# Attention and two feed-forward layers in one kernel: load times, longer waits for other engines, an early table load and an earlier verdict in the order of side work

## The chip, the cores and the metric

One Trainium2 chip, one of its cores. The time is device microseconds (us) of one launch, the median of several runs. Engines are named as in the profile: PE is TensorE's matmul and PEld its weight load, DVE is VectorE, ACT is ScalarE, POOL is GpSimd, SP is SyncE, whose queue issues the loads and stores.

## What is computed

Soft-capped attention (2 batches, 12 heads, 448 positions, 64 per head), then a feed-forward layer with relu squared (768 to 2048 to 768) on 896 tokens, then another of the same size with silu. All inputs are float32.

```python
scores = scale * np.matmul(q, k.transpose(0, 1, 3, 2))
scores = cap * np.tanh(scores / cap)
scores = scores - np.max(scores, axis=-1, keepdims=True)
attn = np.exp(scores)
attn = attn / (np.sum(attn, axis=-1, keepdims=True) + 1e-09)
x = np.matmul(attn, v)                      # then to (896, 768)
h = x @ w_in;   r = np.maximum(h, 0.0);  x = (r * r) @ w_out
h = x @ w2_in;  g = h * (1.0 / (1.0 + np.exp(-h)));  out = g @ w2_out
```

## The kernel before

**Two ways through.** `run(attention_bounded, "f", F16)` computes all of it with feed-forward operands split into a float16 high and low part, and takes samples on the way that tell whether that was good enough (`Watch`). `Watch.judge` puts them together on DVE (eight small operations, lines 244 to 251), `Watch.add_up` sums over partitions with a small matmul (line 254) and three DVE operations (255 to 257) to one number, `ok`. Each engine reads it into a register (`values_load`, line 1337, an instruction TENSOR_LOAD on each of the five). Only if it is not 1 does a second, general program run.

**Attention** (to about 86 us) fills TensorE with float32 products, ACT with tanh and exp.

**The feed-forward layers.** A layer's first product is w_in ("a" in layer one, "c" in layer two), its second w_out ("b", "d"). Each product is three float16 matmuls: high by high, high by low, low by high. Weights come as *words*: tiles of 128 x 768 float64 numbers (768 KB) loaded by SP into three raw buffers (`load_to`, line 275). A word is *turned* into float32 (`turn_steps`): ACT (POOL for the first four) copies the top half into a buffer of zeros (`head`, line 339), DVE shifts the rest under it (`shift`, line 342), and the shift's end lets SP load word i + 3 into the raw buffer. The zeros buffers are three: one for words 0 to 7, two in turn for the others. Then a word is *split* into high (ACT, line 366) and low (DVE, line 206) in a slot `hl`; there are 13 slots, the last three in a pool that opens after attention. Most products of four blocks use seven multiplications in place of eight (`Pair`, and the last stage of layer two, lines 1289 to 1338): sums and differences of words and of operands are formed on DVE (lines 391, 846), and the products go p1, p5, p6, p2, p7, p3, p4. p6 and p2 wait for the copy k1 of p1's bank, p7 for the copy or sum k2 of p6's, p3 for k5. The first pair of layer two goes in another order (`first`), with p7 straight behind p6. The first four columns of layer one (`plain`) use eight.

**Who decides the order.** [...] Program order on ACT and DVE is made at build time by a planner (`Stream`): a `Step` has an engine, a cost from its columns, steps that it depends on, a gate and a due time. TensorE's work moves a clock (`chunk`), and while an engine's planned clock lies behind it, the open step with the earliest due time is put out, of the urgent ones (`late`) or the first six of the background (`bg`). The copies and sums that free a bank (`ends`) are put out when their product is. `open` takes a step whose dependencies on other engines ended HOP = 0.21 us ago by the plan. The plan knows neither the weights' loads nor the reload of the activation table, and starts all engines at 0 when attention ends (`begin`). What TensorE wants and isn't yet put out is forced (`need`, `run_first`).

**Last stage of layer two.** Two groups of two pairs each. Sums go into `yf`, which holds layer two's first results, loaded back from a spill in DRAM (line 1248) as soon as layer two's input is no longer read. The judgement stands behind p7 of the last group, the small matmul and the read behind p3.

Of the kernel before, what the change touches and what calls it, by code (L numbers as in the profile page):

```python
# [26 lines left out]
def softcap_attention_relu2_silu(  # L27
# [12 lines left out]
    nc = tc.nc  # L40
# [139 lines left out]
    HOP = 0.21  # L180
    SLACK = 0.3

# [76 lines left out]
    class Stream:  # L259


        def __init__(self, plan, tag, wpool, dt, watch):
            self.todo = plan
            self.tag, self.wpool, self.dt, self.watch = tag, wpool, dt, watch
            self.nslots, self.nwords, self.nraw = (10, 4, 3) if watch else (5, 4, 3)
            self.nrests = 4 if watch else NHR
            self.nfirst, self.nslots = self.nslots, self.nslots + (3 if watch else 0)
            self.raw, self.hl, self.ready, self.freed = [], {}, {}, {}
            self.turned, self.slots, self.rests, self.order, self.u = [], [], [], [], {}
            self.words, self.read = [], {}  # L270
            self.bg, self.late = {"A": [], "D": [], "P": []}, []
            self.clock, self.now = {"A": 0.0, "D": 0.0, "P": 0.0}, 0.0
            self.steps, self.done = self.plan(), []

        def load_to(self, i):
            while len(self.raw) < min(i + 1, len(self.todo.items)):
                src, name = self.todo.items[len(self.raw)]
                raw = self.wpool.tile([128, WT * 8], I8, tag="raw", bufs=self.nraw, name=f"raw_{name}{self.tag}")
                nc.sync.dma_start(raw, src)
                self.raw.append(raw)  # L280

        def slot(self, i):
# [36 lines left out]
        def turn_steps(self, i):  # L319

            k = 0 if i < 8 or not self.watch else 1 + i % 2
            before = [j for j in range(i) if (0 if j < 8 or not self.watch else 1 + j % 2) == k]

# [4 lines left out]
            def top():  # L330
                return zeros[:, 0] if k == 0 else self.zeros[:, k - 1]

# [16 lines left out]

            a = Step("P" if i < 4 else "A", 280 if i < 4 else 1.4 * WT, head, [self.turned[j] for j in {*before[-1:], *range(max(0, i - self.nraw), max(0, i - self.nraw + 1))}])  # L350
            b = Step("D", WT, shift, [a], self.room)
# [84 lines left out]
        def begin(self):  # L436
# [4 lines left out]
            for st in self.steps:  # L441
                self.bg[st.eng].append(st)
            self.clock = dict.fromkeys(self.clock, 0.0)
            for st in self.done:
                st.end = 0.0

        def run(self, st):
            for d in st.deps:
                if d.end is None:
                    self.run_first(d)  # L450
            t = max([self.clock[st.eng]] + [d.end + (HOP if d.eng != st.eng else 0) for d in st.deps])
            st.fn()
            st.end = self.clock[st.eng] = t + st.cost
# [11 lines left out]
        def open(self, st, now, eng):  # L465
            if any(d.end is None or d.end + (HOP if d.eng != eng else 0) > now for d in st.deps):
                return False
# [383 lines left out]
    def feed_forward(ws, x0, x1_of, ytile, gpool, qpool, tag, dt, power, ones):  # L851
# [324 lines left out]
        for ph in range(len(phases["a"])):  # L1176
# [7 lines left out]
            if ph == len(phases["a"]) - 1:  # L1184
                x1 = x1_of(ws, y1)

            def seed1(acc, n, u):
# [22 lines left out]
        for ph in range(len(phases["c"])):  # L1210
# [93 lines left out]
            for es, p in [(es, p) for es in groups for p in ("p1", "p2", "p5", "p6", "p7", "p3", "p4")]:  # L1304
                for m, e in [(m, e) for m in range(MN) for e in es]:
# [22 lines left out]
                    else:  # L1328
                        ws.chunk(UNIT / 4)
                if p == "p7" and es == groups[-1]:  # L1330
                    for i in (ws.todo.where["d", 0, e] for e in es):
                        ws.get((i, "r"))
                    ws.finish()
                    watch.judge(capt)
                if p == "p3" and es == groups[-1]:
                    watch.add_up(ones[0], bank("judge"))
                    verdict.append(nc.values_load(watch.ok.bitcast(I32), min_val=0, max_val=0x3F800000))
        ws.finish()
# [135 lines left out]
    def run(attention, tag, dt):  # L1474
        narrow = dt == F16
        power = POWER if narrow else dict.fromkeys(POWER, 0)
        with ExitStack() as pools:
# [34 lines left out]
            if watch:  # L1512
                ws.zeros = gpool.tile([128, 2, WT], I32, tag="zeros", name=f"zeros{tag}")
                nc.gpsimd.memset(ws.zeros, 0)
# [59 lines left out]
```

## Time and profile before

| what | us |
|---|---|
| median of 3 runs | 515.94 |
| lowest, highest | 513.95, 517.15 |
| the profiled execution's own time | 513.88 |
| its span, first to last instruction | 512.0 |
| PE busy in it | 493.8 |
| DVE, ACT, POOL busy | 389.4, 344.9, 32.7 |

A row of the timeline gives start, length, engine, line, operation, what it writes and reads, and in brackets how long its engine stood idle before it and which instruction's end let it go. Buffer numbers are left out of some names: `zerosf<-raw_wa5f` is the top half of word 5 of w_in, `hl_51f` a slot's 51st use, `p_6df` a bank of the last stage's second group. A busy PE counts a matmul from start to end, and matmuls overlap.

### The profile page before, as it was taken

To read this page: it belongs to the slowest core of one execution; us is meant where nothing else is said; L and a number is where in the kernel's file an instruction comes from. 1 tells how busy PE (TensorE), PEld (TensorE's weight loads), DVE (VectorE), ACT (ScalarE), POOL (GpSimd) and SP (SyncE) were. 2 spreads that over 40 slices of the span, in tenths; PEclk is the share of its full clock that TensorE was granted. 3 is DMA by queue.
4 is the path that set the end of the run, shared out by engine and by line. 5 is a ranking of instruction groups with operands and counts; after the bars stand their busy time and mean duration, and the time that the engine had idled before them with its cause. 6 is when DMAs were issued, how large, how long until landed. Compare 5 with 4: busy or idle time off the path is not lost.

```text
span 512.0 us, 7109 instructions
## 1 busy us (share of the span) xinstructions
PE 493.8 (96%) x2608; PEld 237.6 (46%) x2608; DVE 389.4 (76%) x754; ACT 344.9 (67%) x540; POOL 32.7 (6%) x33
## 2 busy tenths in 40 slices
PE   8999999998999999999999997999999999998994
PEld 4233333454545555555555554455555555554551
DVE  0888999989989998457988977787043289988853
ACT  6999896679689984249887679897243487871200
POOL 1103554300000000000000000000000000000000
PEclk9999999999999999999999999999999999999999
DMA  7756553333356745515241114653335132232023
GB/s 250 259 151 172 181 155 96 98 140 137 125 184 222 238 158 181 189 51 196 91 156 62 63 61 133 231 192 123 116 115 180 55 123 64 61 124 92 2 100 122
DMA packets 22386, 69.76 MB, mean 136 GB/s; under 512 B 2886, under 2 KB 14150, under 8 KB 22342
## 3 DMA queue, kind: packets, MB, share of 16 engines
q1 hardware_dynamic: 22308, 69.22, 40.7%
q8 instruction: 22, 0.36, 0.3%
q14 instruction: 22, 0.18, 0.1%
q0 software_dynamic: 32, 0.00, 0.0%
q10 hardware_dynamic: 2, 0.00, 0.0%
HBM read 63.64 MB, written 5.54 MB: 135 GB/s over the span
## 4 chain that ended last, share of the span: by engine, by line
PE 69%; DVE 15%; ACT 8%; DMA 5%; issue 2%; SPq 0%; DVEq 0%; ACTq 0%
PE px L623 4%; PE p_6df L896 3%; PE yb_1f L896 3%; PE yb_4f L896 3%; PE yb_0f L896 3%; PE yb_5f L896 3%; PE yb_2f L896 3%; PE yb_3f L896 3%; PE s_A L604 2%; PE p_4df L896 2%; DMA yf<-spill 2%; PE yd_3f L896 2%; PE yd_2f L896 2%; PE yd_5f L896 2%; PE yd_4f L896 2%
## 5 line engine op out<-in xcount | busy, mean ns | idle before, releaser
L612 ACT ACTIVATE e_B<-s_B 128x896 f32<-128x896 f32 x18 | 15.9, 917 | 4.1 <-PE s_B L604 3.8
L612 ACT ACTIVATE e_A<-s_A 128x896 f32<-128x896 f32 x18 | 15.9, 918 | 3.7 <-PE s_A L604 3.4
L708 ACT ACTIVATE e_B<-e_B 128x896 f32<-128x896 f32 x18 | 16.5, 954 | 0.0
L708 ACT ACTIVATE e_A<-e_A 128x896 f32<-128x896 f32 x18 | 16.5, 955 | 0.0
L1254 DVE SCALAR_TENSOR_TENSOR yf<-p_6df,yf 128x448 f32<-128x448 f32 x15 | 9.2, 623 | 7.7 <-PE p_6df L896 7.7
L206 DVE SCALAR_TENSOR_TENSOR hl_63f<-u_62f,hl_63f 128x768 f16<-128x768 f32 x1 | 1.0, 958 | 17.4 <-ACT hl_63f L366 17.4
L643 DVE TENSOR_TENSOR total<-total,e_C 64x896 f32<-64x896 f32 x11 | 12.9, 1172 | 0.4
L206 DVE SCALAR_TENSOR_TENSOR hl_67f<-u_67f,hl_67f 128x768 f16<-128x768 f32 x1 | 1.0, 958 | 14.3 <-ACT hl_67f L366 14.3
L639 DVE TENSOR_TENSOR total<-total,e_A 128x896 f32<-128x896 f32 x6 | 8.8, 1472 | 0.3
L206 DVE SCALAR_TENSOR_TENSOR x1f<-yaf,x1f 128x448 f16<-128x448 f32 x12 | 7.4, 620 | 2.2 <-ACT x1f L835 2.2
L1254 DVE SCALAR_TENSOR_TENSOR yf<-p_4df,yf 128x448 f32<-128x448 f32 x15 | 8.9, 613 | 0.0
L835 ACT ACTIVATE x1f<-yaf 128x448 f16<-128x448 f32 x11 | 6.2, 568 | 3.8 <-DVE yaf L846 3.7
L846 DVE TENSOR_TENSOR yaf<-yaf 128x448 f32<-128x448 f32 x12 | 7.2, 621 | 1.2 <-ACT yaf L835 1.1
L339 ACT ACTIVATE zerosf<-raw_wb_7f 128x768 f16<-128x768 bf16 x2 | 2.1, 1074 | 7.9 <-DMA raw_wb_7f<-in_moe_w_out 4.2
L637 DVE TENSOR_TENSOR total<-e_A,e_A 128x896 f32<-128x896 f32 x6 | 6.6, 1101 | 0.6 <-ACT e_A L708 0.6
L835 ACT ACTIVATE ycf<-yd_4f 128x448 f32<-128x448 f32 x2 | 1.1, 543 | 8.0 <-PE yd_4f L896 8.0
L637 DVE TENSOR_TENSOR total<-e_B,e_B 128x896 f32<-128x896 f32 x5 | 6.5, 1293 | 0.0
L835 ACT ACTIVATE ycf<-yd_0f 128x448 f32<-128x448 f32 x2 | 1.1, 543 | 7.8 <-PE yd_0f L896 7.8
L896 PEld LDWEIGHTS <-hl_5f 128*128 128x128 f16 x36 | 3.5, 97 | 5.8 <-issue 2.8
L696 DVE RECIPROCAL r<-r 128x448 f32<-128x448 f32 x2 | 5.9, 2952 | 0.1
L896 PE MATMUL p_6df<-yformsf,hl_78f 128*128 128x448 f16 x18 | 4.4, 352 | 1.6 <-DVE ok L257 1.6
L366 ACT ACTIVATE hl_79f<-u_79f 128x768 f16<-128x768 f32 x1 | 0.8, 843 | 7.4 <-DVE u_79f L342 7.4
(1836 smaller groups left out, 1653.7 us busy)
## 6 DMA issues: line engine op xcount, KB each, us to landing
spill<-ycf SPq DMA_DIRECT2D x12, 224.0 KB, 1.9
yf<-spill SPq DMA_DIRECT2D x12, 224.0 KB, 5.3
out<-yf SPq DMA_DIRECT2D x12, 224.0 KB, 2.0
rb<-scratch SPq DMA_DIRECT2D x10, 224.0 KB, 4.0
raw_wb_0f<-in_moe_w_out SPq DMA_DIRECT2D x2, 768.0 KB, 5.8
raw_wb_1f<-in_moe_w_out SPq DMA_DIRECT2D x2, 768.0 KB, 4.4
raw_wb_2f<-in_moe_w_out SPq DMA_DIRECT2D x2, 768.0 KB, 6.8
raw_wb_3f<-in_moe_w_out SPq DMA_DIRECT2D x2, 768.0 KB, 5.5
```

The source lines that it names most:

```text
L206: nc.vector.scalar_tensor_tensor(lo, x, scale, hi, op0=ALU.mult, op1=ALU.subtract, accum_out=watch.low() if see else None)
L604: nc.tensor.matmul(sp[:, j, :S] if b is None else sp[head(b), j, :S], lhsT=qk[head(j), 1, 128 * c : min(128 * c + 128, S)], rhs=qk[head(j) ...
L612: nc.scalar.activation(t, sp[:, :, :S], AF.Tanh, scale=scale_s)
L623: nc.tensor.matmul(px[i][head(j), :S], lhsT=v_m[:, 3 * j + int(x[1])] if b is None else pr.vc[m][head(b), j], rhs=e[:, j] if b is None els ...
L637: nc.vector.tensor_tensor(t, ex[m, x[0] + "0"], e, op=ALU.add)
L639: nc.vector.tensor_tensor(total[i], total[i], e, op=ALU.add)
L643: nc.vector.tensor_tensor(t, t, ex[m, "C"][head(b)], op=ALU.add)
L708: nc.scalar.activation(ex[m, x], ex[m, x], AF.Exp, scale=scale_c)
L835: return Step("A", cols, lambda: nc.scalar.activation(at(out), at(src), func, scale=scale), list(deps))
L846: return Step(eng, cols, lambda: e.tensor_tensor(at(out), at(x), at(y), op=op), list(deps))
L896: nc.tensor.matmul(acc, lhsT=w(e_w, kk), rhs=x(e_x, kk), start=first and i == 0, stop=last and i == len(n) - 1, skip_group_check=more,)
L1254: return Step("D", S, lambda: nc.vector.scalar_tensor_tensor(yb, acc, to_y, yb, op0=ALU.mult, op1=ALU.add), list(deps))
```

## The change

Seven edits, all to the planner's knowledge or to where a step stands:

- `loaded`: each load gets a time at which the plan expects it, 4.5 us after the step that issued it and at least 3.1 us after the load before; the copy of a top half has it as its gate.
- CAUTION: `open` asks for 0.6 us, not 0.21, since a dependency on another engine ended.
- `begin` starts DVE's clock at 2.2. `run` lets a step's planned start wait for its gate.
- Zeros buffers: two in all. Odd words from 9 on use the second, the others the first.
- Slots: 14 in place of 13, four in the late pool, in the room that the zeros buffer gave up.
- A silu activation of one element is put out as a late ACT step in layer one's last phase, before its output products.
- `judge` moves behind p5 of the last group (with the splits that it wants), `add_up` behind p6, the read behind p7.

```diff
-    SLACK = 0.3
+    SLACK, CAUTION = 0.3, 0.6
+    LOAD, NEXT_LOAD = 4.5, 3.1
...
-            self.nfirst, self.nslots = self.nslots, self.nslots + (3 if watch else 0)
+            self.nfirst, self.nslots = self.nslots, self.nslots + (4 if watch else 0)
...
+                last = self.loaded[-1] if self.loaded else 0.0
+                self.loaded.append(max(self.at + LOAD, last + NEXT_LOAD) if self.loading else -1.0)
...
-            k = 0 if i < 8 or not self.watch else 1 + i % 2
-            before = [j for j in range(i) if (0 if j < 8 or not self.watch else 1 + j % 2) == k]
+            k = i % 2 if i > 7 and self.watch else 0
+            before = [j for j in range(i) if k == (j % 2 if j > 7 and self.watch else 0)]
...
+            def loaded():
+                return self.loaded[i] if i < len(self.loaded) else -1.0 if i < self.nraw else None
...
-            a = Step("P" if i < 4 else "A", 280 if i < 4 else 1.4 * WT, head, [self.turned[j] for j in {*before[-1:], *range(max(0, i - self.nraw), max(0, i - self.nraw + 1))}])
+            a = Step("P" if i < 4 else "A", 280 if i < 4 else 1.4 * WT, head, [self.turned[j] for j in {*before[-1:], *range(max(0, i - self.nraw), max(0, i - self.nraw + 1))}], loaded)
...
-            self.clock = dict.fromkeys(self.clock, 0.0)
+            self.clock = {"A": 0.0, "D": 2.2, "P": 0.0}
...
+            if st.gate is not None:
+                t = max(t, st.gate() or 0.0)
+            self.at = t + st.cost
...
-            if any(d.end is None or d.end + (HOP if d.eng != eng else 0) > now for d in st.deps):
+            if any(d.end is None or d.end + (CAUTION if d.eng != eng else 0) > now for d in st.deps):
...
+                ws.later(Step("A", 1400, lambda: nc.scalar.activation(warm, warm, AF.Silu)))
...
-                if p == "p7" and es == groups[-1]:
+                if p == "p5" and es == groups[-1]:
                     for i in (ws.todo.where["d", 0, e] for e in es):
-                        ws.get((i, "r"))
+                        ws.need(ws.ready[i + 1], ws.ready[i, "r"])
                     ws.finish()
                     watch.judge(capt)
-                if p == "p3" and es == groups[-1]:
+                if p == "p6" and es == groups[-1]:
                     watch.add_up(ones[0], bank("judge"))
+                if p == "p7" and es == groups[-1]:
                     verdict.append(nc.values_load(watch.ok.bitcast(I32), min_val=0, max_val=0x3F800000))
...
-                ws.zeros = gpool.tile([128, 2, WT], I32, tag="zeros", name=f"zeros{tag}")
+                ws.zeros = gpool.tile([128, WT], I32, tag="zeros", name=f"zeros{tag}")
```

## Rows read from the trace of the kernel before

**Rows 1.** The page: busy time by engine, and the chain that ended last
```profile
PE 493.8 (96%) x2608; PEld 237.6 (46%) x2608; DVE 389.4 (76%) x754; ACT 344.9 (67%) x540; POOL 32.7 (6%) x33
PE 69%; DVE 15%; ACT 8%; DMA 5%; issue 2%; SPq 0%; DVEq 0%; ACTq 0%
```

**Rows 2.** Stage table: stretch, then per engine busy us (x instructions); clock; DMA
```profile
84.00:152.00 68.00, 63.81 (x333) 31.89 (x330) 62.78 (x120) 53.50 (x94) 5.69 (x6) 1.00 0.43 145
406.00:458.00 52.00, 52.00 (x277) 26.89 (x275) 47.38 (x117) 41.33 (x72) 0.00 (x0) 1.00 0.24 79
```

**Rows 3.** TensorE's waits: for whom, us in total, times, longest
```profile
PE ac0f L896 <- ACT u2c0f L835: 2.7, 1, 2.7
PE p_6df L896 <- DVE ok L257: 1.6, 1, 1.6
PE p_4df L896 <- DVE yf L1254: 1.5, 2, 1.3
PE aa4f L896 <- ACT ca4f L835: 1.2, 1, 1.2
PE ha_0f L896 <- ACT ha_0f L835: 1.1, 1, 1.1
PE yb_0f L896 <- DVE ga3f L206: 0.8, 1, 0.8
PE yb_0f L896 <- ACT ga3f L835: 0.6, 1, 0.6
PE yb_1f L896 <- DVE ga3f L206: 0.5, 1, 0.5
```

**Rows 4.** Timeline, first layer: start, us, engine, line, tiles [idle before <-releaser]
```profile
86.53 2.44 PE L896 MATMUL ha_0f<-x0f,hl_0f 128*128 128x448 f16 x12
...
95.21 0.58 ACT L835 ACTIVATE x0f<-x_c11f 128x448 f16<-128x448 f32 x1 [4.53 <-DVE x_c11f L697]
...
114.53 1.07 ACT L339 ACTIVATE zerosf<-raw_wa5f 128x768 f16<-128x768 bf16 x1 [2.82 <-DMA raw_wa5f<-in_moe_w_in]
...
138.72 1.08 ACT L339 ACTIVATE zerosf<-raw_wa9f 128x768 f16<-128x768 bf16 x1 [2.24 <-DMA raw_wa9f<-in_moe_w_in]
```

**Rows 5.** Timeline, first pair of layer two
```profile
306.81 0.84 ACT L366 ACTIVATE hl_51f<-u_51f 128x768 f16<-128x768 f32 x1 [1.57 <-PE cc0f L896]
...
307.56 0.35 PE L896 MATMUL ac0f<-x_c11f,hl_39f 128*128 128x448 f16 x1
...
307.66 1.28 ACT L835 ACT_TABLE_LOAD   x1
...
308.95 0.54 ACT L835 ACTIVATE c11c0f<-cc0f 128x448 f32<-128x448 f32 x1
...
310.01 0.53 ACT L835 ACTIVATE u2c0f<-ac0f 128x448 f32<-128x448 f32 x1
```

**Rows 6.** Timeline around the verdict, VectorE and TensorE
```profile
490.49 0.63 DVE L1254 SCALAR_TENSOR_TENSOR yf<-p_6df,yf 128x448 f32<-128x448 f32 x1 [0.51 <-PE p_6df L896]
...
493.69 0.73 PE L896 MATMUL p_6df<-yformsf,hl_78f 128*128 128x448 f16 x3
...
497.84 0.13 DVE L244 TENSOR_SCALAR signs<-capt 1x1 f32<-1x1 f32 x1
...
499.59 0.16 DVE L251 TENSOR_TENSOR squares<-squares,within 128x1 f32<-128x1 f32 x1
```

**Rows 7.** Line 1337, the verdict's read: count, duration in ns min/median/max, first and last start
```profile
L1337 PEldq TENSOR_LOAD <-ok x1: 712/712/712, 501.7 to 501.7; - x1
```

**Rows 8.** Timeline of VectorE: a split that waits for its slot, a sum for the spill
```profile
376.92 0.96 DVE L206 SCALAR_TENSOR_TENSOR hl_63f<-u_62f,hl_63f 128x768 f16<-128x768 f32 x1 [17.39 <-ACT hl_63f L366]
...
462.88 0.62 DVE L1254 SCALAR_TENSOR_TENSOR yf<-c_4df,yf 128x448 f32<-128x448 f32 x1 [4.08 <-DMA yf<-spill]
```

**Rows 9.** Stage table of line 206 alone (lower halves and their reads), VectorE
```profile
406.00:458.00 52.00, 23.34 (x72) 1.00 0.24 79
458.00:484.00 26.00, 8.55 (x22) 1.00 0.24 82
```

More of the change, by code (lines that the diff above doesn't have):

```diff
@@ L270, in __init__ @@
             self.words, self.read = [], {}
+            self.loaded, self.at = [], 0.0
             self.bg, self.late = {"A": [], "D": [], "P": []}, []
@@ L330, in top @@
             def top():
-                return zeros[:, 0] if k == 0 else self.zeros[:, k - 1]
+                return zeros[:, 0] if k == 0 else self.zeros
+            def loaded():
+                return self.loaded[i] if i < len(self.loaded) else -1.0 if i < self.nraw else None
             def head():
```

## The prediction

> **What bounds the kernel now.** I read the page first (busy shares and the chain that ended last), then the stage table, then the list of what TensorE waited for, and then the timeline around each of these waits. TensorE is busy 96% of the span and the chain is TensorE for 69% [rows 1]; its granted clock is 1.00 in every stage quoted [rows 2], so no term below is one of the clock. A gain can only come out of TensorE's idle time and of the tail. The list of its waits says where that idle time is: after attention, eight entries of 0.5 us or more hold 10.0 us [rows 3]. They are 2.7 (first pair of layer two), 1.6 (the verdict), 1.5 (the last stage), 1.2 (the first paired products), 1.1 and 0.8 + 0.6 + 0.5 = 1.9 (first layer's plain products). No entry is for a weight split. The change works on the order in which ScalarE (ACT) and VectorE (DVE) get side work, so its worth is the sum of what becomes of these eight, less new waits that another order makes.
>
> **First layer, start: 1.1 and 1.9 us.** TensorE begins the layer at 86.53. ACT, next in order with x0f, stands idle 4.53 us until DVE's last normalisation lets it go at 95.21 [rows 4]. The planner took DVE as free at 0: by its own costs 0.55 + 2.90 + 0.55 + 0.21 it had x0f ready at 4.2, and the trace has it at 95.21 - 86.53 = 8.7. With DVE set to 2.2 it is planned at 6.4, so some 2.2 of the 4.53 us should be filled with work that now stands behind it. The wait of 1.1 us [rows 3] is for a bank whose relu is queued behind; 2.2 us more is enough: 1.1 gained. Next, ACT stands 2.82 us before the top half of word wa5, whose load has not landed, and the relus for ga2 and ga3 are behind it [rows 4]. TensorE's 1.9 us of waits for ga3 follow. The new gate plans that half for 4.5 us after the load's issue, so relus go first. It could give back all 1.9, or nothing if DVE, which is busy 62.78 of 68 us in this stage [rows 2], is what is late (two of the three waits name DVE); I take 1.5. **Sum 2.6, from 1.1 to 3.0.** A loss from words turned later I leave out here, as no wait now is for a weight.
>
> **First paired products: 1.2 us.** The copy ca4f is late after ACT has lost 2.24 us to the load of wa9 [rows 4]. The same gate removes it; but DVE's words for the same ACT work are as late, so I take **0.9, from 0 to 1.2**.
>
> **Silu's table: 2.68 us.** The load takes 1.28 us and runs while TensorE waits for u2c0f; before it ACT waited 1.57 us for cc0f and then did hl_51f, 0.84 us [rows 5]. hl_51f takes the buffer of word 38 (13 slots), which is read until cc0f is done; with 14 slots it takes that of word 37, free earlier. If only the table load goes, u2c0f ends 1.28 us sooner. If hl_51f goes too, u2c0f is bound by the product's end: last matmul 307.56 + 0.35 = 307.91, some 0.02 to start, 0.53 for the copy, 0.05 to restart, a wait of about 0.64, thus 2.04 gained. I take **1.6, from 1.28 to 2.04**. At its new place, behind the first layer's last products, the load costs ACT the same 1.28 us and a one-element activation. The output products that follow read words and g tiles made before, and want the last pair's g only eight units on: that hides it. Without this cover it would cost TensorE 1.28 us there. It issues no DMA.
>
> The trace shows no pause between hl_51f's end (306.81 + 0.84), the load at 307.66 and the silu at 308.95: a switch costs 1.28 us [rows 5]. The Trainium skill (ScalarE: Activation LUTs, What ACT_TABLE_LOAD costs) has 1283 ns for the load, which agrees, and a DRAIN of about 1380 ns beside it, which this trace doesn't show; by its 2.66 us this term would be 2.66 and 1.06 more than I take. The row decides.
>
> **Verdict: 1.6 us.** Now judge starts when the p7 sums are done (497.84), ends at 499.59 + 0.16 = 499.75, and TensorE waits for the verdict behind its sum [rows 6]. After, it starts behind the third p5 sum, 490.49 + 0.63 = 491.12, and by the same 1.91 us ends at 493.03. What is late next: the p6 sums queued behind it on DVE. The first would end at 493.03 + 0.62 = 493.65, and p7's first product, which wants it, starts at 493.69 now; the sum's small matmul stands before it, so I see it as just in time (up to 0.5 us lost if not). Behind three sums of 0.62 the verdict is ready near 495, over two us before p7's sums are done (497.84 now), where each engine reads it. That read takes TensorE's queue 0.712 us [rows 7] and nothing covers it but what is already in the array. 1.6 - 0.7 = **0.9, from 0.4 to 1.6**. DVE's own read falls between p7's and p3's sums, where no product waits for it; SP's stands before the p3 stores, which are not due before their sums; ACT and POOL have nothing left behind it. The tail after the last matmul is unchanged.
>
> **Fourteenth slot, last stage: 1.5 us.** DVE stood 17.39 us for hl_63f, whose slot was held by words of layer two's first output stage, and in the last stage TensorE waits for sums while DVE does weight splits as long as that one, 0.96 us; there DVE had stood 4.08 us for the spill's load, which the planner doesn't know before or after [rows 8]. One slot more lets one split go into that idle time: **0.5, from 0 to 0.96**. The second zeros buffer that pays for it was one of three; the first is now used on, so word 8 waits for word 7, in a stretch with room.
>
> **New waits.** A changed greedy order makes some. The trace has nothing that prices them but its own: 10.0 / 8 = 1.25 us each; I take one of 0.9, between that and the smallest (0.5); from 0 up to the slower rival. The caution of 0.6 us has no instruction of its own.
>
> **Sum.** 2.6 + 0.9 + 1.6 + 0.9 + 0.5 = 6.5; less 0.9 = 5.6 us. Against the profiled execution, 513.88 us (its span 512.0 and 1.9 around it), that is 508.3. That execution is at the low edge of the runs (513.95 to 517.15); taken off their median of 515.94 it gives **510.3 us**, my forecast. If all goes to its upper end: 3.0 + 1.2 + 2.0 + 1.6 + 1.0 = 8.8, with no new wait: 507.1.
>
> **The rivals.**
> - All upper ends: 507.1, or a little under with the rest of the waits. Chance 0.08.
> - The waits for loads only move: ACT does relus first, but then turned words come late, and DVE, at 62.78 of 68 us, is the bound of the first layer. Then only table and verdict are left, 1.6 + 0.9 = 2.5: 513.4. For it: two of the three ga3 waits name DVE. Against: ACT's idle time comes before the relus that DVE waits for. Chance 0.21.
> - The table load does not stay away. If Relu isn't in silu's set, the relus still open at the new place bring the first table back, and silu's load returns at 307. The term of 1.6 is lost: 511.9. In this trace Copy and Square run in both layers with no reload; of Relu under silu's table it shows nothing. Chance 0.07. (The Trainium skill, ScalarE: Activation LUTs, Table sets, says relu and copy are in every set: by that the rival falls.)
> - Slower: DVE starves in layer two's second half. From 406 to 458 it is busy 47.38 of 52 us, so 4.6 are free [rows 2], and 36 of its steps there (72 instructions with their reads) follow an ACT step [rows 9]. The caution holds each back by up to 0.6 - 0.21 = 0.39 us in the plan; where DVE then gets a sum that waits for TensorE in its place, that time is lost. All 36 lose 14.0 us, and with the 11 such steps from there to 484, where DVE's idle time lies behind the spill's load, 18.3; less 4.6 free, less 6.0 gained by the other terms: 7.7 slower, 523.6. It decides against the change from (4.6 + 6.0) / 0.39 = 27 steps on, and by more than 1% (5.2 us) from 41. Against it: the caution moves a plan, not an instruction, and DVE mostly has other work. Chance 0.12.
>
> **How the numbers follow.** The forecast as told (net gain of some 3.5 to 8) has 0.52. What a measurement of this kernel can tell from no change is about 1%, 5.2 us: faster by more means under 510.8, and the forecast is just there. Of its 0.52 I put 0.41 under that line and 0.11 within 1%. Faster: 0.41 + 0.08 = 0.49. Same: 0.11 + 0.21 + 0.07 + 0.04 of the last rival = 0.43. Slower: 0.08, the rest of it. The range reaches from 506, the upper ends and the runs' own spread, to 516.5, which takes in the second and third rivals and leaves the slower one out; the forecast alone would be 507 to 513.
>
> **What would show it.** Right: no ACT idle time of over 1 us before a top half that names a load; x0f's wait near 2.3; no table load near 307 and TensorE's wait there 0.6 to 1.4; one table load near 260; the verdict's wait near 0.7; hl_63f's split done before 370. Wrong: the same number of table loads plus one or more after 260; waits of TensorE for weights (hl) or for sums between 406 and 470 that are not there now; a wait at p7's first product. If the span falls by less than 2.5 us with table and verdict as told, the step on loads failed.

## The result, and the profile after

The changed kernel takes **503.4 us** (median of 4, 502.91 to 504.16) against 515.92 (513.95 to 517.15): a ratio of 0.976, 95% interval 0.973 to 0.980. The forecast was 510.3 with a range from 506.0, so the sign was right and the gain of 12.5 us was over twice the 5.6 that I had summed. The kernel before also varies more from execution to execution than the changed one; experiment 6 is on that.

The page after, busy time by engine and the chain that ended last:

```profile
PE 492.3 (98%) x2608; PEld 237.9 (47%) x2608; DVE 392.1 (78%) x770; ACT 340.9 (68%) x524; POOL 31.6 (6%) x33
PE 93%; ACT 2%; DMA 1%; DVE 1%; issue 1%; SPq 0%; DVEq 0%
```

Against [rows 1] TensorE's work is the same, 2608 matmuls; ScalarE (ACT) has 16 instructions fewer and VectorE (DVE) 16 more; the share of TensorE (PE) in the chain went from 69% to 93%. What went is idle time between its matmuls. The stage table after, stretches as in [rows 2]:

```profile
84.00:152.00 68.00, 68.00 (x362) 34.58 (x359) 64.51 (x127) 53.12 (x88) 5.40 (x6) 1.00 0.43 146
406.00:458.00 52.00, 51.72 (x274) 26.70 (x273) 45.03 (x112) 35.84 (x63) 0.00 (x0) 1.00 0.26 84
```

From 84 to 152 us TensorE now never stands, and 362 of its matmuls fall into these 68 us where 333 had; VectorE, which I had weighed as the bound there, went from 62.78 to 64.51 us of 68 and delivered all the same. TensorE's waits after (for whom, us in total, times, longest):

```profile
PE p_4df L906 <- DVE yf L1265: 1.8, 2, 1.5
PE idle L91 <- DVE idle L88: 1.1, 1, 1.1
PE ac0f L906 <- ACT u2c0f L845: 0.6, 1, 0.6
PE s_A L614 <- ACT e_A L622: 0.3, 1, 0.3
PE aa12f L906 <- ACT ca12f L845: 0.2, 1, 0.2
```

Of the eight entries of [rows 3] two are left: the last stage's sums, and 0.6 for the first silu. The entries for the engines' start and for `s_A` are attention's, and were there before. To put each place in us, I took every start of a matmul that comes more than 0.19 us (their usual distance) behind the one before, from the first layer on, in both traces. What is over the 0.19 us is the gap. Such a gap is longer than the entry in the list of waits, which counts from the end of the matmul before, 0.35 us after its start: by 0.35 - 0.19 = 0.16 us each (2.84 and 2.68 at the first silu before, 0.79 and 0.63 after).

| place | before | after | gained | my sum had |
|---|---|---|---|---|
| a bank for ha_0f | 1.2 | 0 | 1.2 | 1.1 |
| ga3f, five gaps | 2.5 | 0 | 2.5 | 1.5 |
| ca4f | 1.4 | 0 | 1.4 | 0.9 |
| first silu, u2c0f | 2.8 | 0.8 | 2.0 | 1.6 |
| verdict, with its small matmul | 1.7 | 0.1 | 1.6 | 0.9 |
| sums of the last stage | 2.1 | 2.1 | 0.0 | 0.5 |
| gaps of 0.1 to 0.4 in both layers (nine, now three) | 2.1 | 0.7 | 1.4 | not there |
| new waits | | 0 | 0 | -0.9 |
| sum | | | **10.1** | **5.6** |

TensorE's last end moved from 506.0 to 496.4 while its first layer began 0.55 us later (87.08, was 86.53), 10.2 us in all; the profiled executions differ by 9.7 (513.88 and 504.16).

ScalarE in the first layer after, from its timeline:

```profile
87.80 0.58 ACT L845 ACTIVATE x0f<-x_c10f 128x448 f16<-128x448 f32 x1 [1.01 <-DVE x_c10f L707]
...
117.44 1.05 ACT L346 ACTIVATE zerosf<-raw_wa5f 128x768 f16<-128x768 bf16 x1
...
133.13 1.07 ACT L346 ACTIVATE zerosf<-raw_wa9f 128x768 f16<-128x768 bf16 x1
```

The 4.53, 2.82 and 2.24 us of [rows 4] are 1.01, none and none. wa5's top half stands 2.9 us later in the span than before and no longer waits; `x_c11f`, for which ACT had stood 4.53, is now copied on VectorE.

Silu's table and the first silu:

```profile
257.05 0.58 ACT L845 ACTIVATE ga15f<-c21a14f 128x448 f16<-128x448 f32 x1
257.65 1.28 ACT L1196 ACT_TABLE_LOAD   x1
258.94 0.20 ACT L1196 ACTIVATE warm<-warm 1x1 f32<-1x1 f32 x1
...
302.59 0.35 PE L906 MATMUL ac0f<-x_c11f,hl_39f 128*128 128x448 f16 x1
...
302.98 0.54 ACT L845 ACTIVATE u2c0f<-ac0f 128x448 f32<-128x448 f32 x1
...
303.57 0.35 PE L906 MATMUL ac0f<-x_c0f,hl_40f 128*128 128x448 f16 x1 [0.63 <-ACT u2c0f L845]
```

The load of 1.28 us stands at 257.65 and no more where [rows 5] has it; `hl_51f` is gone from there too (its high part is made at 296.5). The wait of 0.63 is what I had worked out for that case (0.64): the last matmul ends at 302.59 + 0.35 = 302.94, and u2c0f follows. ScalarE's last relu (`c21a14f`, 255.58), its square (256.46) and the copy into `ga15f` (257.05) all stand ahead of the load, so the rival of a table that comes back was never put to the test.

The verdict, VectorE, TensorE and the weight side's read:

```profile
482.47 0.62 DVE L1265 SCALAR_TENSOR_TENSOR yf<-p_6df,yf 128x448 f32<-128x448 f32 x1 [0.51 <-PE p_6df L906]
483.01 0.13 DVE L245 TENSOR_SCALAR signs<-capt 1x1 f32<-1x1 f32 x1
...
485.99 0.74 PE L906 MATMUL p_6df<-yformsf,hl_78f 128*128 128x448 f16 x3
...
488.84 0.73 PE L906 MATMUL p_6df<-yformsf,hl_81f 128*128 128x448 f16 x3
489.41 0.73 PE L906 MATMUL p_6df<-gc13f,hr_60f 128*128 128x448 f16 x3
```
```profile
L258 DVE TENSOR_REDUCE ok<-signs x1: 160/160/160, 486.7 to 486.7; 1x1 f32<-1x19 f32 x1
...
L1349 PEldq TENSOR_LOAD <-ok x1: 486/486/486, 486.9 to 486.9; - x1
L1349 DVEq TENSOR_LOAD <-ok x1: 804/804/804, 489.6 to 489.6; - x1
```

The judgement begins behind the third p5 sum and p7's first product (485.99) follows the small matmul without a wait, as forecast. But the read, which in the program stands behind p7, is done at 486.9 + 0.49 = 487.4, while p7's matmuls run on to 489.4: the queue of the weight side was over 2 us ahead of the array and stood at the read when `ok` came.

VectorE, against [rows 8]:

```profile
368.86 0.96 DVE L207 SCALAR_TENSOR_TENSOR hl_64f<-u_64f,hl_64f 128x768 f16<-128x768 f32 x1 [15.93 <-ACT hl_64f L373]
...
454.94 0.62 DVE L1265 SCALAR_TENSOR_TENSOR yf<-c_4df,yf 128x448 f32<-128x448 f32 x1 [4.38 <-DMA yf<-spill]
```

hl_63f is now split at 348.1, and it is the next word, hl_64f, that waits for a slot; the wait for the spill is as long as before (4.38, was 4.08).

### The profile page after: what moved, and what is told of

It is laid out like the page before. It is cut to its first block, busy times and chain, and to the rows that moved or that the text cites. A ratio compares the mean times of both kernels' runs of the same rounds, so it can differ in the third digit from the quotient of the medians.

```text
span 502.3 us, 7110 instructions
## 1 busy us (share of the span) xinstructions
PE 492.3 (98%) x2608; PEld 237.9 (47%) x2608; DVE 392.1 (78%) x770; ACT 340.9 (68%) x524; POOL 31.6 (6%) x33
## 4 chain that ended last, share of the span: by engine, by line
PE 93%; ACT 2%; DMA 1%; DVE 1%; issue 1%; SPq 0%; DVEq 0%
PE px L633 7%; PE p_6df L906 4%; PE yb_5f L906 4%; PE yb_3f L906 4%; PE yb_1f L906 4%; PE yb_0f L906 4%; PE yb_4f L906 4%; PE yb_2f L906 4%; PE s_B L614 3%; PE s_A L614 3%; PE ha_0f L906 3%; PE ha_1f L906 3%; PE p_4df L906 2%; PE yd_3f L906 2%; PE yd_5f L906 2%; PE yd_4f L906 2%
## 5 line engine op out<-in xcount | busy, mean ns | idle before, releaser
L236 ACT ACTIVATE junk<-x0f 128x896 bf16<-128x896 f16 x6 | 5.7, 947 | 0.3
L906 PE MATMUL p_4df<-yformsf,hl_72f 128*128 128x448 f16 x18 | 4.4, 352 | 1.5 <-DVE yf L1265 1.5
L649 DVE TENSOR_TENSOR total<-total,e_B 128x896 f32<-128x896 f32 x5 | 5.5, 1091 | 0.4
```

What stands on the lines that cost most here:

```text
L649: nc.vector.tensor_tensor(total[i], total[i], e, op=ALU.add)
L906: nc.tensor.matmul(acc, lhsT=w(e_w, kk), rhs=x(e_x, kk), start=first and i == 0, stop=last and i == len(n) - 1, skip_group_check=more,)
```

## Experiments

Kernels named u_ undo something in the changed kernel, a_ add one part to the kernel before; the others change the changed kernel. us are medians with the lowest and highest run, ratios are to the kernel before. The changed kernel's own runs spread over 1.3 us, so differences under that between two of its variants are not told apart by time; there the trace speaks.

**1. The three edits on the order, in the changed kernel.** u_load:
```diff
-...range(max(0, i - self.nraw), max(0, i - self.nraw + 1))}], loaded)
+...range(max(0, i - self.nraw), max(0, i - self.nraw + 1))}])
```


> The changed kernel without the gate on a word's load (the copy of a top half is planned as if its word were always there). Theory 1, each edit gives back just the waits that I put down to it: TensorE's waits before about 150 us come back, some 1.9 us at the ga3 products and 1.2 us at the first paired products, so about 3 to 4 us slower than the changed kernel, near 507, and ACT waits of over 2 us for a load of wa5 or wa9 stand in the trace again. Theory 2, the caution and the later start of VectorE's clock carry the first layer and the loads are hidden anyway: under 1 us slower, with ACT waits for loads but no TensorE wait behind them.


u_caution:
```diff
-d.end + (CAUTION if d.eng != eng else 0) > now
+d.end + (HOP if d.eng != eng else 0) > now
```


> The changed kernel with 0.21 us in place of 0.6 us in the test of what an engine may take. Theory 1, the caution only changes which of several ready steps comes first: within 1 us of the changed kernel. Theory 2, it is what took away the small waits of 0.1 to 0.4 us in both layers (1.4 us together in the kernel before, 0.5 in the changed one) and part of the first layer's: 1.5 to 3 us slower, with small TensorE waits for ACT copies (ca, cc) in the trace again.


u_dstart:
```diff
-self.clock = {"A": 0.0, "D": 2.2, "P": 0.0}
+self.clock = {"A": 0.0, "D": 0.0, "P": 0.0}
```


> The changed kernel with VectorE's clock started at 0, not 2.2, when attention ends. Theory 1: ACT waits some 4 us for the last normalisation again and TensorE's wait of about 1.1 to 1.2 us for the third bank of the first layer comes back: 1 us slower. Theory 2, the caution or the load gates already put other work first: no change within 0.3 us, no TensorE wait near 100 us.


u_load_caution has the first two of these diffs:


> The changed kernel without the load times and without the caution. Theory 1, each stands in for the other: with both gone the first layer's waits are back, 3 to 5 us slower than the changed kernel (507 to 508), although one alone costs 0.5 and 1.2. Theory 2, the later start of VectorE's clock, the slot and the zeros buffers are enough: under 2 us slower.


u_three has all three:


> The changed kernel without the load times, without the caution and with VectorE's clock started at 0: of the edits on the order only the fourteenth slot stays. If the three stand in for each other and at least one is needed: the first layer's waits come back (ha_0f 1.1, ga3f 1.9, ca4f 1.2 in part), 505.5 to 507.5 us. If the slot's order alone carries the first layer: no PE wait over 0.5 us before 170 and 503.4 to 504.5. The kernel before with the slot alone kept about 2.1 us of waits there (yb_1f 0.7, ha_0f 0.5, ca4f 0.4, yb_0f 0.4) with one look, so I lean to the first, at about 505.5.

| kernel | us | ratio, 95% | TensorE's first-layer waits in the list, us |
|---|---|---|---|
| u_load | 503.87 (503.36 to 504.33) | 0.978, 0.975 to 0.981 | none |
| u_caution | 504.58 (503.39 to 505.06) | 0.979, 0.975 to 0.982 | 0.2 |
| u_dstart | 503.97 (503.37 to 504.23) | 0.978, 0.975 to 0.982 | none |
| u_load_caution | 504.14 (503.33 to 505.45) | 0.977, 0.971 to 0.983 | 0.2 |
| u_three | 508.31 (507.14 to 508.89) | 0.983, 0.977 to 0.990 | 2.1 |

Each edit undone alone costs 0.5 to 1.2 us, which the spread hides, and the pair that was tried 0.7; all three cost 4.9 us, more than I expected. (The changed kernel's own list has 0.2 in this layer.) The trace shows why for the start. In u_load_caution ACT stands again for wa5's load; in u_three it stands also for x0f:

```profile
87.30 0.58 ACT L845 ACTIVATE x0f<-x_c10f 128x448 f16<-128x448 f32 x1 [1.01 <-DVE x_c10f L707]
...
111.16 1.07 ACT L346 ACTIVATE zerosf<-raw_wa5f 128x768 f16<-128x768 bf16 x1 [3.03 <-DMA raw_wa5f<-in_moe_w_in]
```
```profile
95.48 0.58 ACT L845 ACTIVATE x0f<-x_c11f 128x448 f16<-128x448 f32 x1 [4.00 <-DVE x_c11f L707]
...
114.52 1.07 ACT L346 ACTIVATE zerosf<-raw_wa5f 128x768 f16<-128x768 bf16 x1 [2.54 <-DMA raw_wa5f<-in_moe_w_in]
```

With VectorE's later start alone (first fence) ACT loses 3.03 us to a load and TensorE feels nothing, because ACT did not lose the 4 us before. With all three gone (second fence) both losses are back, and TensorE's timeline in u_three has waits again:

```profile
101.65 2.43 PE L906 MATMUL ha_0f<-x0f,hl_2f 128*128 128x448 f16 x12 [0.53 <-ACT ha_0f L845]
...
123.18 0.35 PE L906 MATMUL yb_1f<-ga3f,hl_5f 128*128 128x448 f16 x1 [0.65 <-DVE ga3f L207]
```

The other half is in a_load (experiment 2), where ACT stands for x0f and not for wa5:

```profile
94.93 0.58 ACT L845 ACTIVATE x0f<-x_c11f 128x448 f16<-128x448 f32 x1 [4.00 <-DVE x_c11f L707]
```

There the waits for ga3f and ca4f are gone and 0.5 us for ha_0f is left, as in u_three. So ha_0f's wait comes with the loss at x0f alone, but for ga3f and ca4f the first layer has room for one late ACT, not for two: I had priced each of these gaps by the one ACT wait in front of it.

**2. The same in the kernel before.** a_load adds `loaded` and its constants alone, a_caution the 0.6 alone:
```diff
-...range(max(0, i - self.nraw), max(0, i - self.nraw + 1))}])
+...range(max(0, i - self.nraw), max(0, i - self.nraw + 1))}], loaded)
```


> The kernel before with the load times alone (each word's load in the plan, the gate on the copy of a top half, a step's start waiting for its gate). Theory 1: it takes TensorE's waits at ga3 (1.9 us) and at the first paired products (1.2 us) away and nothing at the first silu or the verdict: 3 to 4 us faster than the kernel before, near 512. Theory 2, without the caution and VectorE's later start the order stays bad in the first layer: under 1.5 us faster.


```diff
-d.end + (HOP if d.eng != eng else 0) > now
+d.end + (CAUTION if d.eng != eng else 0) > now
```


> The kernel before with the caution of 0.6 us alone. So far: without the load times the changed kernel is only 0.5 us slower, and the load times alone give the kernel before 3.4 us. Theory 1, the edits stand in for each other in the first layer: the caution alone also takes TensorE's waits for ga3 (1.9 us) and for ca4f (1.2 us) away, 2.5 to 4 us faster than the kernel before (near 512). Theory 2, it does so only with VectorE's later start: under 1.5 us faster, ga3 waits still there. By both, VectorE is behind in the last stage as in the kernel with 13 slots: splits of the last four words later than in the kernel before.


a_load: 511.79 us (509.24 to 513.14), 0.994, 0.991 to 0.997. Its first-layer list keeps 0.5 us, so the load times alone do nearly what VectorE's start does alone (u_load_caution). a_caution: 512.13 (510.71 to 513.82), 0.992, 0.990 to 0.995. Its waits:

```profile
PE ac0f L896 <- ACT u2c0f L835: 2.7, 1, 2.7
PE p_4df L896 <- DVE yf L1254: 1.8, 1, 1.8
PE p_6df L896 <- DVE hl_79f L206: 1.7, 1, 1.7
PE p_6df L896 <- DVE ok L257: 1.6, 1, 1.6
...
PE yb_0f L896 <- DVE ga3f L206: 1.0, 1, 1.0
```

ha_0f, ca4f and half of ga3f are gone, and there is a wait for a weight split, hl_79f, that neither the kernel before nor the changed one has. That is the mechanism of my slower rival, a VectorE that gets late in layer two's second half, at 1.7 us and not at 14 or 18.

**3. The fourteenth slot.** u_slot takes it away, a_slot gives it to the kernel before (with the zeros buffers as in the change):
```diff
-self.nslots + (4 if watch else 0)
+self.nslots + (3 if watch else 0)
```


> The changed kernel with 13 slots in place of 14 (zeros buffers as changed). Theory 1, the slot moves work out of the stretch after 406 us and hl_51f out of the way of the first silu: 0.2 to 1 us slower, TensorE's wait at u2c0f up from 0.63 to about 1.4 us, the wait of the last stage for sums (1.5 us) larger by up to 0.95. Theory 2, the slot has no worth, since the last stage's wait is for the spill's load in both kernels: within 0.3 us.

> The kernel before with two zeros buffers and 14 slots alone. With 13 slots the changed kernel is 4.4 us slower: 0.6 at u2c0f, 1.1 in small waits for ACT copies, 1.7 for a weight split of the last stage. Theory 1, the slot has that worth by itself: 2 to 4 us faster than the kernel before (near 512), the u2c0f wait at 2.0 or below and the last stage's waits under 1. Theory 2, most of it is work that the caution makes late and the slot takes back: 0 to 1.5 us faster, with the last stage's wait of 1.3 us for sums still there.


u_slot: 507.83 (507.54 to 508.21), 0.986, 0.982 to 0.989. a_slot: 509.71 (509.35 to 510.01), 0.987, 0.982 to 0.993. By the medians it is the largest single part, 4.4 us undone and about 6 alone, where I had 0.5. Between profiled executions it is 4.1 undone (508.21 and 504.16) and 4.4 alone (513.88 and 509.49), no more than a_load's 4.6 (509.24); the rest of the 6 fits the clock of experiment 6, as all four runs of a_slot are at 0.997 to 0.999. u_slot's waits:

```profile
PE p_6df L906 <- DVE hl_79f L207: 1.7, 1, 1.7
PE p_4df L906 <- DVE yf L1265: 1.7, 1, 1.7
PE ac0f L906 <- ACT u2c0f L845: 1.3, 1, 1.3
```

The wait for hl_79f is in the three kernels that have the caution without the slot (a_caution, u_slot, u_slot_silu) and in no other: in these the split of hl_79f ends 20.3 us behind VectorE's first sum of the last stage, in the four without slot and caution 17.8. VectorE splits hl_76f at 446.6 in the changed kernel and at 464.4 in u_slot:

```profile
446.55 0.95 DVE L207 SCALAR_TENSOR_TENSOR hl_76f<-u_76f,hl_76f 128x768 f16<-128x768 f32 x1
```
```profile
464.39 0.95 DVE L207 SCALAR_TENSOR_TENSOR hl_76f<-u_76f,hl_76f 128x768 f16<-128x768 f32 x1
```

In the changed kernel it lies 8 us before VectorE's first sum of the last stage (454.94), in u_slot 8 us behind it (456.69), among the sums. So the slot does what I gave it 0.5 us for, one more split ahead of the sums, but its worth is elsewhere. Counted by starts of matmuls, u_slot loses 1.9 us at hl_79f, the wait that the caution makes and the slot keeps away, 0.6 at the first silu and 1.2 in small gaps of both layers, and gains 0.3 at the sums. a_slot's gain has 2.0 us of first-layer gaps in it, at ha_0f, ga3f and ca4f; since a_slot brings the change's zeros buffers along, which u_slot keeps, the buffers' own share of that was not tested.

**4. Silu's table.** u_silu takes the early silu out, a_silu puts it alone into the kernel before, u_slot_silu takes out both it and the slot:
```diff
-ws.later(Step("A", 1400, lambda: nc.scalar.activation(warm, warm, AF.Silu)))
```


> The changed kernel without the early silu activation. Theory 1: the table load returns near 302 us, in front of the first silu, and since hl_51f is done before, u2c0f comes 1.28 us later: TensorE's wait of 0.63 us grows to about 1.9, 1.3 us slower (near 504.7). Theory 2, the planner and the fourteenth slot had already taken the load off the path: under 0.4 us slower. No ACT work at 258 us becomes free that TensorE wanted, by both.

> The kernel before with the early silu alone. My prediction's step: u2c0f comes 1.28 us sooner, the wait of 2.7 becomes 1.4, all else stays, 515.5 - 1.3 = 514.2 by median. If the long wait is also what lowers the granted clock behind it in some executions: a narrower spread and mean clocks of 0.997 to 0.999 throughout, and 2 to 4 us less by median, 511.5 to 513.5. If the table only moves the wait (the buffer of hl_51f becomes the bound): the wait stays near 2.7 and the time too.

> The changed kernel with 13 slots and without the early silu. If the two overlap at the first silu (the slot moves hl_51f away, so that the table load falls into time that is free anyway): the undoing costs more than the sum of the single ones, 4.4 + 0.8 = 5.2, because the wait for u2c0f goes from 1.3 to about 2.7: 509.2 to 510.5 us. If they add: 508.6. If a wait of 2.7 us there lowers the granted clock in some executions: spread over 2 us and mean clocks of 0.990 to 0.996 among the runs; else a spread near 1 us and 0.997 to 0.999.

| | us | wait for u2c0f |
|---|---|---|
| before | 515.92 | 2.7 |
| a_silu: table alone | 513.04 (511.06 to 516.2) | 1.3 |
| a_slot: slot alone | 509.71 | 1.2 |
| changed kernel without both (u_slot_silu) | 510.60 (509.19 to 511.38) | 2.7 |
| without the slot (u_slot) | 507.83 | 1.3 |
| without the table (u_silu) | 504.21 (503.62 to 504.59) | 0.7 |
| changed kernel | 503.4 | 0.6 |

Either edit alone takes the wait from 2.7 to about 1.3, as forecast for the table; a_silu's ratio is 0.995 (0.991 to 0.999), some 2.6 us and not 1.3, with the wide spread that experiment 6 is on. But with the slot in place the table costs TensorE almost nothing where it was: in u_silu the load runs at 300.03, in time that ACT would have spent waiting for `cc0f`:

```profile
300.03 1.28 ACT L845 ACT_TABLE_LOAD   x1
301.32 0.54 ACT L845 ACTIVATE c11c0f<-cc0f 128x448 f32<-128x448 f32 x1
```

Undone singly the table is worth 0.8 us at most (the runs overlap), undone with the slot the two are worth 7.2, more than 0.8 + 4.4. Of the excess of 2.0 the profiled execution has some 1.6 in slower matmuls behind the wait of 2.7 (experiment 6). The early silu is cover for a late `hl_51f`, and the other way round.

**5. The verdict and its read.** u_judge puts judgement, small sum and read back to p7 and p3, the last part of the change's diff turned round; j_read leaves the judgement early and moves only the read ahead, to right behind the small sum:
```diff
 if p == "p6" and es == groups[-1]:
     watch.add_up(ones[0], bank("judge"))
-if p == "p7" and es == groups[-1]:
     verdict.append(nc.values_load(watch.ok.bitcast(I32), min_val=0, max_val=0x3F800000))
```


> The changed kernel with the judgement where it was (judge behind p7, the sum and the read of the verdict behind p3). Theory 1, the read is hidden because TensorE's queue comes to it two products ahead of the array and finds the verdict just written: the wait of 1.6 us for the verdict comes back, 1.6 us slower (near 505). Theory 2, what is gained at the verdict is partly paid elsewhere (the p6 sums behind the judgement): 1.0 us or less.

> The changed kernel with the read of the verdict right behind the small sum, at the end of p6, not at the end of p7. Theory 1, the read is hidden in the changed kernel because 3.4 us of products stand between sum and read: here TensorE's queue stands until the p6 sums and the three small operations are done, about 0.9 us after the sum's matmul, and for the read's 0.5 to 0.7: a TensorE wait of 1.2 to 1.8 us at p7's first product, about 1.5 us slower (near 505). Theory 2, what is queued in the array covers it: within 0.4 us.


u_judge: 505.33 (504.34 to 505.9), 0.981, 0.978 to 0.984; the wait of 1.6 is back, and the time is 1.9 us more. j_read: 505.21 (504.34 to 506.4), 0.979, 0.973 to 0.985, with

```profile
PE p_6df L906 <- DVE ok L258: 1.4, 1, 1.4
```

at p7's first product. So it isn't the early judgement alone that pays: the 3.4 us of p7's matmuls between the small sum and the read hide both the three operations on VectorE and the read.

**6. The spread of the kernel before.** Over all its runs it took 512.2 to 519.7 us, with a mean granted clock of 0.989 to 0.999; the changed kernel's four are at 0.997 to 0.999. The stage table of the kernel before, of a_caution and of u_slot_silu around the first silu, whose wait of 2.7 us all three have:

```profile
308.00:312.00 4.00, 1.41 (x8) 0.77 (x8) 1.86 (x4) 3.37 (x7) 0.00 (x0) 1.00 0.02 6
312.00:316.00 4.00, 4.00 (x23) 2.07 (x22) 3.42 (x8) 3.62 (x7) 0.00 (x0) 1.00 0.62 190
```
```profile
304.00:308.00 4.00, 1.32 (x8) 0.58 (x6) 1.60 (x4) 3.95 (x8) 0.00 (x0) 1.00 0.56 190
308.00:312.00 4.00, 4.00 (x14) 1.68 (x13) 2.00 (x4) 2.58 (x4) 0.00 (x0) 0.57 0.04 10
312.00:316.00 4.00, 4.00 (x23) 2.08 (x22) 3.71 (x8) 2.31 (x5) 0.00 (x0) 1.00 0.59 199
```
```profile
304.00:308.00 4.00, 1.73 (x8) 0.82 (x8) 1.51 (x4) 3.96 (x8) 0.00 (x0) 0.94 0.59 201
308.00:312.00 4.00, 4.00 (x15) 1.74 (x14) 2.50 (x4) 1.61 (x3) 0.00 (x0) 0.64 0.22 25
```

In two of the three the 4 us behind the wait have a granted clock of 0.57 and 0.64, so for most of it the lower of the two levels, 1.2 of 2.4 GHz, and 14 or 15 matmuls in place of 23: 8 or 9 times 0.19, some 1.6 us lost. In the profiled execution of the kernel before it stayed at 1.00, and in a_load's too, which has the same wait. The time goes with the clock: of the 51 executions of the kernel before that were run beside the experiments, the 19 with a mean of 0.998 or 0.999 have a median of 513.9 us, the 11 at 0.993 or below 517.6, and a straight line through all has 0.49 us for each 0.001. a_load_silu takes away the first layer's waits but for 0.5 us and halves the one for u2c0f, and does nothing for the verdict and the last stage (the diffs of a_load and of the early silu, in the kernel before):


> The kernel before with the load times and the early silu, no other edit: TensorE's waits in the first layer go but for some 0.5 us, that for u2c0f goes from 2.7 to 1.3, those for the verdict (1.6) and the sums of the last stage (1.3 to 1.8) stay. If the long waits of the first layer and of the first silu are what lowers the granted clock behind them: all executions at 0.997 to 0.999, a spread of under 2 us, median 507.5 to 509. If the waits for the verdict and the sums do it as well: executions at 0.992 to 0.996 among them, spread of 3 us or more, median 508.5 to 511.


It takes 509.17 us (507.88 to 509.63), 0.989, 0.985 to 0.993, clocks 0.996 to 0.999: a spread of 1.8 us in six runs, where a_load has 3.9 in six (0.993 to 0.999) and a_silu 5.1 in ten (0.992 to 0.999). The waits for the verdict and for the last stage's sums are still in it, 1.6 and 1.5, and do not widen it. For a_silu no profile shows where the clock fell; its longest waits before the last stage are 1.1 to 1.3, and a_slot, with somewhat shorter ones, stays at 0.997 to 0.999 in four runs. So that the long waits bring the lower clock is seen in two executions and fits the spreads, but a_silu's spread is not explained by it. (The mean counts the time behind the last matmul too, where the profiles show it low, so 0.001 or 0.002 in one run say little.)

**7. What is left.** b_spill loads the spill in the order in which its blocks are summed, in the changed kernel; b_spill_p3 also puts the rest of the p3 products ahead of p7's, in `first`, the order of the first pair of layer two:
```diff
-for n, b in ((1, 1), (0, 1), (0, 0), (1, 0)):
+for n, b in ((0, 0), (1, 1), (0, 1), (1, 0)):
```


> The changed kernel with the spill's twelve loads in the order in which their sums want them (block 0,0 first, not 1,1). All twelve are issued only when layer two's input is read for the last time, so the first sums wait for the seventh load, landed 8.6 us after the first issue. Theory 1, that order makes VectorE late by 4.4 us and TensorE by 1.8 us in the last stage: with block (0,0) first the sums start near 451.5, TensorE's two waits of 0.28 and 1.5 us go, 1.5 to 2 us faster than the changed kernel (near 501.6). Theory 2, VectorE's weight splits in that stage are the bound whatever the spill does: under 0.5 us. Theory 3, loads of the other blocks come late in turn: TensorE waits at p7 or p4 in place of p5 and nothing is gained.


```diff
-("p3", range(1)), ("p6", late), ("p7", range(n)), ("p3", range(1, n)), ("p4", range(n)),
+("p3", range(1)), ("p6", late), ("p3", range(1, n)), ("p7", range(n)), ("p4", range(n)),
```


> The changed kernel with the spill's loads in the order of use and the rest of the p3 products ahead of p7's. If the stores and sums at the end gain room by it: up to 0.5 us under the 501.7 of the load order alone. If the last sums now stand behind other work, or the sums that p3 wants are not there yet: same or up to 1 us more. I expect the same within 0.4 us.


b_spill: **501.68 us** (501.55 to 501.88), 0.974, 0.971 to 0.977, the lowest of all; every run is under the changed kernel's lowest. VectorE's first sum of the last stage there:

```profile
450.66 0.62 DVE L1265 SCALAR_TENSOR_TENSOR yf<-c_4df,yf 128x448 f32<-128x448 f32 x1 [0.27 <-PE c_4df L906]
```

It waits for its product and not for the load, and TensorE's waits of 1.8 for these sums are off its list. b_spill_p3: 502.85 (502.58 to 503.03), 0.973, 0.967 to 0.979, 1.2 us more. Its list no longer has 0.6 for u2c0f, but 0.4 for `cc6f` and

```profile
PE ac0f L906 <- DVE s5c0f L856: 1.0, 1, 1.0
```

before p4's first product, which writes the bank that p7 has just filled and so waits for p7's sum: p7 now stands straight ahead of it. The expectation looked for the effect at the end of the kernel, but the order that was edited is used near 300 us. I expected the same time; that was a miss.

## Why the prediction was right or wrong

- **Where the time is: right.** I said that a gain could only come out of TensorE's idle time, place by place; the gaps that went (10.1 us), less the layer's later start (0.55), are the profiled gain (9.7) to within 0.2. What failed is the size, in the terms and in the step from one execution to the median. By the table the terms were 4.5 us too small: 1.6 in the first layer and first paired products, 0.4 at the table, 0.7 at the verdict, 0.9 of new waits that did not come and 1.4 of gaps left out, less 0.5 for the last stage.
- **First layer and first paired products, 2.6 + 0.9: too small, 5.1.** Two steps failed. One is the discount: I took 1.5 of 1.9 because two of three waits name VectorE at 62.78 of 68 us, and 0.9 of 1.2, 0.7 us in all; VectorE delivered in time at 64.51. The other is that I took an entry in the list of waits as what the wait costs: these entries hold 4.2 us, the gaps from start to start 5.1, as each is 0.16 longer than its entry. And I gave each edit the gap behind the one ACT wait it removes; experiments 1 and 2 show that for ga3f and ca4f two losses of ACT have to come together, and that VectorE's start alone, or the other two edits together, take enough of them away. The rival "the waits only move" is refuted by the 68.00 of 68 us.
- **Silu's table, 1.6: 2.0, my own upper case.** The condition that I named for it, hl_51f gone too, came true. The attribution was wrong: with the slot the table is nearly free, and it is the pair that carries the 2 us (experiment 4). The 1.28 us of the row held at the new place; the DRAIN of about 1380 ns that the Trainium skill has beside it (ScalarE: Activation LUTs, What ACT_TABLE_LOAD costs) is not seen there either: the silu follows 1.29 us after the load's start.
- **Verdict, 0.9: 1.6.** The failed step is "nothing covers it but what is already in the array": that cover was over 2 us long, more than the read, which took 0.49 us in place of 0.712. Put ahead of p7 (j_read), the verdict costs 1.4.
- **Fourteenth slot, 0.5: mis-sized.** The gap that I gave it, in the last stage, did not move (2.1 and 2.1). Its worth undone, 4.4 us by the medians, is mostly at hl_79f (1.9), at the first silu (0.6) and in small gaps (1.2) (experiment 3). I had looked for it where VectorE had stood longest for a slot, and not at every step whose place a free slot changes.
- **New waits, -0.9: none.** The one that the caution makes, hl_79f at 1.7, is covered by the slot. So the slower rival had a real mechanism, but at one wait, and the change brought its own remedy.
- **Gaps under 0.5 us: left out, 1.4.** I had cut the list at 0.5; six of nine such gaps went.
- **From profile to median.** The sum gave 508.3 on the profiled execution, which took 504.16 after: 4.1 us of the miss are the terms. The other 2.8 came with the step to 510.3: I took a gain read from one execution off the median of runs that lay 2.0 above it, and after, the profiled run lies 0.8 above its median. The failed step here is "no term below is one of the clock", which I had read from that one execution. Against the executions of the kernel before at 0.998 or 0.999 (513.9) the changed kernel gains 10.5 us, close to the 10.1 of the gaps; the other two of the 12.5 go with the lower clock that executions of the kernel before have and the changed kernel's four have not (experiment 6). Which of the waits bring it in each execution stays open.
- **Chances.** The nearest case, all terms at their upper ends (507.1), had 0.08, and even that was 3.7 too high. I had allowed terms to lose independently; here they lean on each other, and with all of them in place all but the slot's last-stage term came to their upper ends or above.

## What to carry to other kernels

Undo edits one by one and in groups: parts that stand in for each other look nearly worthless singly (0.5 to 1.2 us each, 4.9 together), and parts that cover each other look dear singly or not at all. When the engine that sets the end waits for a planner's order, take the whole of its idle time at the places that the change touches as the likely gain, small gaps included and measured from start to start, and keep discounts for places where the trace shows another bound. Take that gain off an execution of the same granted clock, not off a median over several. A program's place of a register read says little: ask how far its queue runs ahead of the engine.

## What the runs showed of the hardware

- A register read that the program puts behind 18 matmuls was done in the queue of the weight loads at 487.4 us, 1.8 us before the last of them started (488.84 + 2 x 0.19): its 0.49 us were free. The same read took 0.71 us in the kernel before [rows 7] and in u_judge.
- After a wait of 2.7 us TensorE's granted clock was 0.57 and 0.64 over the next 4 us in two profiled executions and 1.00 in two others (the kernel before, a_load); behind waits of 1.2 to 1.9 us no profiled execution of any kernel here shows such a fall.
